# Attention and expert layer on one core: seven products from the fourth batch on, weight sums over two plain layers, splits on ScalarE

## The chip, the cores and the metric

One Trainium2 chip, one core of it. The time is device microseconds of one execution, the median of several runs. A trace of one profiled execution of the kernel before is at hand; its own time stands beside its span in the table below.

## What is computed

Eight batches of attention with a sigmoid in place of the softmax, then one expert: a product into 2048 columns, an ELU, and a product back to 768.

```python
B, H, S, D = 8, 12, 448, 64            # q, k, v
scores = q @ k.T / sqrt(D) - log(S)    # per batch and head
attn_out = sigmoid(scores) @ v         # x: 3584 tokens x 768
h = x @ w_in                           # 768 x 2048
g = where(h > 0, h, exp(min(h, 0)) - 1)
out = g @ w_out                        # 2048 x 768
```

All inputs and outputs are f32. The kernel splits each f32 operand, scaled by a power of two, into a high and a low f16 part and adds three products (high by high, low by high, high by low).

## The kernel before

**Stages.** The work goes batch by batch. For a batch b there is an *attention stretch* (six pairs of heads, class `Pair`), then a *layer* (x by w_in and the ELU, giving g). The second product of the expert (`moe2`, g by w_out) of batch b-1 is cut into output tiles of 128 tokens by 384 columns, 16 steps of 6 matmuls each, and TensorE runs these steps between the score and value products of the attention stretch of batch b (`fill`). Of the 448 tokens of a batch 384 make three whole tiles; the last 64 of two successive batches share one tile, so the stretches of batches 2, 4, 6 hold eight output tiles (even stretches) and those of 1, 3, 5, 7 hold six (odd stretches). All instructions are issued in an order written out by hand on every engine; batch 0 and the attention of batch 1 follow the string `ORDER`, whose letters each advance one stream of work.

**Layers.** `FAST = 2`: the layers of batches 0 and 1 are plain (`Expert`, `moe1`: 16 tiles of 18 matmuls of 448 columns). From batch 2 on a layer is made of seven products of halves (`FastExpert`, `moe1_fast`: four blocks j of seven products, each of 18 matmuls of 224 columns). For these, x of a pair is evicted as 32-bit data (`evict`, L833) into the place of a part of w_in (`hold`), VectorE makes sums and differences of halves (`differences`, L840 to L859), ScalarE casts them to high parts (`rest`, L872), GpSimd or VectorE makes the low parts (`rest_low`, L878). The places of successive pairs overlap, so that an eviction waits for the low parts of the pair before. `final` scales a pair by GpSimd (L814, L818) ahead of its eviction.

**Weight sums.** The layers of seven products need sums of halves of w_in. `w_in_pieces` makes them on GpSimd in 192 steps (`make`, L342 and L345) and sends them to DRAM (`pieces`): one step every fifth letter of the hand-written order from letter 266 on, four per tile in the plain layer of batch 1, and the rest in the attention stretch of batch 2. `load_piece` brings them back, four per block.

**Preparation.** For a pair that comes some pairs later q, k and v are measured (`greatest`, L220; `greatest_qk`, L570), summed over rows by TensorE (`sums`, L198, into a bank of `pm` or `pav`), scaled (`scales`, L165 to L208 on VectorE and GpSimd, L587, L589, `value_scale` L537 to L547), split into a high part (`split_high`, L625 on GpSimd) and a low part (`split_low`, VectorE, helper line L213), transposed by a DMA (`transposed`) and, for the pair after next, loaded (`load_pair`). Four pairs are prepared in an attention stretch (pairs 1 to 4 of it), two in a layer. `split` (L623) does high and low parts on ScalarE and VectorE; the layer of batch 1 uses it already.

**Order in one pair of an attention stretch:** two score tiles and their sigmoids (L732), high parts (L762, ScalarE) and low parts (L213, VectorE) of the weights `ats`; some steps of `moe2`; the third score tile; row sums, scales and `split_high` of the prepared pair; its sigmoid; the last 64 keys of two pairs (`last_keys`); `final`; `rest` of the pair before, `split_low`, `rest_low`; loads and measurement of the next pair; the other steps of `moe2`; the value products; `evict`.

**Memory.** PSUM tiles are taken by tags: `psc` two of two banks (score tiles, and bank A of the first three blocks of a layer), `pav` one bank, `pm` three. A tile of a tag is reused when its readers have finished.

Of the kernel before, what the change touches and what calls it, by code (L numbers as in the profile page):

```python
# [47 lines left out]
def attention_ffn(  # L48
# [9 lines left out]
    nc = tc.nc  # L58
# [13 lines left out]
    FAST = 2  # L72
    MADE = 265
# [115 lines left out]
    def one_more(tag, name):  # L189
        return ps.tile([P, 512], F32, tag=tag, name=name, bufs=3 if tag == "pm" else None)  # L190
# [141 lines left out]
    unsent, made = [], [0]  # L332
    PIECE_STEPS = NJ * KC * 16

    def w_in_pieces():

        extra = xall[:, NK * 2 * S :]
        free = [extra[:, i * 4 * P : (i + 1) * 4 * P] for i in range(3)]
        ends = [extra[:, 12 * P : 14 * P], spare[:, : 2 * P]]

        def add(dst, x, y, op=ALU.add):
            nc.gpsimd.tensor_tensor(dst, x, y, op=op)  # L342

        def parts(t, hi, lo):
            nc.gpsimd.tensor_copy(hi, t)  # L345
            yield
            add(lo, t, hi, ALU.subtract)
            yield

        def two(t):  # L350
            return t[:, : 2 * P], t[:, 2 * P :]

        def send(j, c, n, hi, lo):
            def run():
                to = pieces[j * 4 + n, :, :, c]
                if lo is None:
                    nc.sync.dma_start(to, hi.rearrange("p (i x) -> p i x", i=2))
                else:
                    nc.sync.dma_start(to[:, 0], hi)
                    nc.sync.dma_start(to[:, 1], lo)  # L360
            unsent.append((made[0], run))

        for j in reversed(range(NJ)):
            for c in range(KC):
                a, b, d = free
                af, bf, df = (t.bitcast(F32) for t in free)
                (h11, l11), (h12, l12), (h21, l21), (h22, l22) = (
                    (wi[:, n, j, 0, c], wi[:, n, j, 1, c]) for n in range(4)
                )
                add(af, h21, l21)  # L370
                yield
                add(bf, af, h11, ALU.subtract)
# [3 lines left out]
                yield from parts(bf, *ends)  # L376
                send(j, c, 2, *ends)
# [6 lines left out]
                yield from parts(af, *two(d))  # L384
                send(j, c, 0, d, None)
                yield from parts(bf, *ends)
                send(j, c, 1, *ends)
                add(bf, h12, bf, ALU.subtract)
# [319 lines left out]
    class Pair:  # L708
# [166 lines left out]
        def rest_low(self):  # L875
            on = nc.vector if self.hp >= NP - 2 else nc.gpsimd
            for (hi, lo), t in self.parts_of:
                on.tensor_tensor(lo, t, hi, op=ALU.subtract)  # L878
# [873 lines left out]
```

## Time and profile before

| | us |
|---|---|
| median of three runs | 1215.45 (1214.18 to 1215.93) |
| profiled execution | 1213.94 |
| span of its trace | 1212.2 |

| engine | busy us | share | instructions |
|---|---|---|---|
| TensorE (PE) | 1130.8 | 93% | 10980 |
| VectorE (DVE) | 874.4 | 72% | 1378 |
| ScalarE (ACT) | 729.0 | 60% | 955 |
| GpSimd (POOL) | 566.8 | 47% | 885 |

The mean granted TensorE clock is 0.979 of full. Busy shares are means over stages with different limits, so the rows below are read stage by stage; "idle before" is the idle time of an engine just ahead of an instruction, with what released it.

### The profile page before, as it was taken

Reading aid. Unit: us, or ns where it says so; the run is one execution under the profiler, and the core shown is the slowest. Engines: PE = TensorE matmul, PEld = TensorE weight load, DVE = VectorE, ACT = ScalarE, POOL = GpSimd, SP = SyncE. Lnnn points to the kernel's source line nnn. Section 1 sums busy time; section 2 is a strip of 40 time slices with the busy share of each in tenths; the row PEclk is TensorE's granted clock in tenths of the full one; section 3 lists DMA queues with packets and bytes.
Section 4 is the critical chain, followed back from the end, with each engine's and each line's share of the span. In section 5 each row is a group of like instructions: output and inputs, shape, how many; then the busy total and the mean of one; then the engine's idle time right before and its main releaser. Section 6 shows DMA issues by size and latency. Waiting matters only on the chain.

```text
span 1212.2 us, 26930 instructions
## 1 busy us (share of the span) xinstructions
PE 1130.8 (93%) x10980; PEld 772.1 (64%) x10980; DVE 874.4 (72%) x1378; ACT 729.0 (60%) x955; POOL 566.8 (47%) x885
## 2 busy tenths in 40 slices
PE   7889888899969999889999999889999999899998
PEld 4334454455636995559766796549866697458965
DVE  4999958967567776787767786787777876766610
ACT  6879758767555466555755557555665467565600
POOL 2357668958967234642356342562236433640000
PEclk9989999999989999999999999999999999999999
DMA  9967554343144551346224552446424462214200
GB/s 275 277 195 217 135 129 106 79 99 87 34 109 95 167 135 38 89 126 178 65 60 93 164 144 47 92 93 174 121 48 93 125 195 47 62 36 151 66 27 27
DMA packets 240044, 136.37 MB, mean 113 GB/s; under 512 B 185008, under 2 KB 217392, under 8 KB 239920
## 3 DMA queue, kind: packets, MB, share of 16 engines
q1 hardware_dynamic: 238848, 134.33, 42.0%
q8 instruction: 86, 1.41, 0.5%
q10 hardware_dynamic: 1072, 0.33, 0.1%
q14 instruction: 38, 0.31, 0.1%
HBM read 98.04 MB, written 17.30 MB: 95 GB/s over the span
## 4 chain that ended last, share of the span: by engine, by line
PE 45%; POOL 18%; DVE 15%; ACT 11%; issue 6%; DMA 4%; SPq 2%; POOLq 0%; DVEq 0%; ACTq 0%
PE po L1238 10%; PE C L1080 6%; PE a L1080 5%; POOL nat L625 5%; PE E L1080 5%; PE ph L987 5%; ACT sg L732 4%; DVE ats L213 4%; PE po_r L1238 3%; PE B L1080 3%; POOL vn L625 3%; PE psc L725 2%; PE pav L794 2%; ACT ats L762 2%; DMA wi<-pieces 2%
## 5 line engine op out<-in xcount | busy, mean ns | idle before, releaser
L1238 PE MATMUL po<-wo,g 128*64 128x384 f16 (+1 forms) x4320 | 403.3, 333 | 0.0
L1238 PEld LDWEIGHTS <-g 128*64 128x64 f16 (+1 forms) x4992 | 302.2, 111 | 157.2 <-issue 25.8
L1080 PEld LDWEIGHTS <-wi 128*128 128x128 f16 x3024 | 287.9, 98 | 6.5 <-DMA wi<-pieces 3.3
L213 DVE SCALAR_TENSOR_TENSOR ats<-sg,ats 128x896 f16<-128x896 f32 x120 | 132.7, 1135 | 72.6 <-ACT ats L762 72.4
L732 ACT ACTIVATE sg<-psc,bias,sc 128x896 f32<-128x896 f32 x126 | 133.9, 1095 | 2.8 <-PE psc L725 2.0
L725 PE MATMUL psc<-qk 64*128 64x448 f16 x756 | 89.3, 359 | 35.8 <-ACT sg L732 35.6
L625 POOL TENSOR_SCALAR nat<-raw,sc 128x384 f16<-128x384 f32 (+1 forms) x99 | 120.2, 1229 | 0.1
L570 POOL TENSOR_TENSOR mx<-mx,half 128x2 bf16<-128x2 bf16 x42 | 24.4, 581 | 196.8 <-DVE mx L220 196.8
L987 PE MATMUL ph<-xall,wi 128*128 128x448 f16 x576 | 114.7, 360 | 0.7 <-DVE e L1013 0.7
L213 DVE SCALAR_TENSOR_TENSOR nat<-raw,sc,nat 128x384 f16<-128x384 f32 (+1 forms) x126 | 83.8, 702 | 41.0 <-POOL nat L625 37.5
L762 ACT ACTIVATE ats<-sg 128x896 f16<-128x896 f32 x120 | 110.0, 951 | 3.5 <-PE pav L794 2.8
L213 DVE SCALAR_TENSOR_TENSOR g<-e,rr,g 128x768 f16<-128x768 f32 (+2 forms) x112 | 91.3, 851 | 16.5 <-ACT g L1144 15.6
L833 ACT ACTIVATE wi<-pav,sc 128x448 f32<-128x448 f32 x30 | 19.0, 634 | 137.6 <-POOL xall L878 87.8
L987 PEld LDWEIGHTS <-wi 128*128 128x128 f16 x576 | 56.3, 100 | 56.8 <-issue 8.3
L725 PEld LDWEIGHTS <-qk 64*128 64x128 f16 x756 | 32.3, 95 | 82.6 <-issue 64.1
L794 PEld LDWEIGHTS <-vn 128*64 128x64 f16 x880 | 52.2, 111 | 49.1 <-issue 18.8
L794 PE MATMUL pav<-ats,vn 128*64 128x448 f16 x720 | 78.8, 358 | 4.9 <-DVE ats L213 2.8
L169 POOL TENSOR_SCALAR sc<-sc 128x3 f32<-128x3 f32 (+1 forms) x48 | 13.9, 290 | 145.6 <-DVE pw L205 145.3
L1080 PE MATMUL C<-xall,wi 128*128 128x224 f16 x720 | 76.9, 259 | 2.3 <-DMA wi<-pieces 2.1
L1080 PE MATMUL a<-xall,wi 128*128 128x224 f16 x720 | 76.9, 259 | 0.0
L1125 ACT ACTIVATE e<-ats,msc 128x448 f32<-128x448 f32 x48 | 32.0, 666 | 62.8 <-DVE ats L1090 62.7
L1238 PE MATMUL po_r<-wo,g 128*64 128x384 f16 (+1 forms) x672 | 64.9, 326 | 0.0
(193 smaller groups left out, 1865.7 us busy)
## 6 DMA issues: line engine op xcount, KB each, us to landing
wi<-pieces SPq DMA_DIRECT2D x96, 384.0 KB, 3.6
wo<-in_moe_w_in_dram SPq DMA_DIRECT2D x8, 1536.0 KB, 7.3
raw<-in_q_dram SPq DMA_DIRECT2D x48, 192.0 KB, 3.7
rv<-in_v_dram SPq DMA_DIRECT2D x48, 192.0 KB, 3.3
raw<-in_k_dram SPq DMA_DIRECT2D x47, 192.0 KB, 3.3
out_dram<-room SPq DMA_DIRECT2D x47, 192.0 KB, 2.3
wo<-in_moe_w_out_dram SPq DMA_DIRECT2D x9, 768.0 KB, 5.4
ats<-in_moe_w_out_dram SPq DMA_DIRECT2D x6, 768.0 KB, 4.7
```

The costliest lines, as they stand in the source:

```text
L213: nc.vector.scalar_tensor_tensor(lo, src, s, hi, op0=ALU.mult, op1=ALU.subtract)
L570: nc.gpsimd.tensor_tensor(mx[:, 5:14:8], mx[:, 9:10].to_broadcast([P, 2]), half, op=ALU.mult)
L625: on.tensor_scalar(to, src, s, None, op0=ALU.mult)
L725: nc.tensor.matmul(psc[:, j, :S], kk[rows[j], o], qq[rows[j], :S], start=(n == 0), stop=(n == len(parts) - 1),)
L732: nc.scalar.activation(to, psc, AF.Sigmoid, bias=bias, scale=self.s_scale)
L762: nc.scalar.mul(hi, sg, 2.0**ATOP)
L794: nc.tensor.matmul(pav[rows[j], :S], vv[i][:, 2 * NC + j if g == NC else j * NC + g], sg[k][:, j], start=(g == 0 and n == 0), stop=(g == N ...
L833: nc.scalar.mul(t[:, : 2 * HS], self.pav[:, :S], self.x_scale)
L987: nc.tensor.matmul(self.ph[f], wi[:, 2 * (f // NQ) + c // KC, f % NQ // 2, wj, c % KC, f % 2 * P :][:, :P], self.xh[c][:, xj], start=(n == ...
L1080: nc.tensor.matmul(bank[:, u * HS : (u + 1) * HS], wi[:, w, at, wj, c, u * P : (u + 1) * P], self.x.piece(x, c, xj), start=begins and u == ...
L1125: nc.scalar.activation(e, h, AF.Exp, scale=self.scale_of(0, j, n))
L1238: nc.tensor.matmul(po[r, :HM], tokens[:, r], wo[:, i, f, wj], start=(n == 0), stop=(n == 3 * NF - 1),)
```

## The change

- `FAST = 3`: the layer of batch 2 and its attention stretch become plain.
- The 192 weight steps leave the hand-written order. A class `Pieces` makes them for given units of 16 steps on a given engine: two units on GpSimd and two on VectorE in the layer of batch 1, four on GpSimd in the attention stretch of batch 2 (one step to every second step of `moe2`), two on GpSimd and two on VectorE in the layer of batch 2. GpSimd's units have one pair of buffers for parts to be sent, VectorE's five (in `ats`).
- The splits of q, k and v go from GpSimd (`split_high`, `split_low`) to `split`, with the high parts on ScalarE; in the attention stretch they come behind the casts of x (`rest`).
- `differences` follows `evict` at once, where it stood ahead of the casts a pair later; the last two pairs' `x_most` comes behind the low parts.
- In the layers of seven products `copied`, `elu`, `high`, `low`, row sums and splits are in another order; the row sums use a bank of `psc`; `load_pair` is issued at the end of a block (in an attention stretch: behind the steps of `moe2`).
- The first pair of a stretch takes 24 steps of `moe2`, and none are kept for behind the last pair.
- In even batches k is loaded ahead of q, so that the last 64 tokens stand at the front of g, and g of every batch is written in one run; the shared output tile reads its two halves from two places.

```diff
-    FAST = 2
-    MADE = 265
+    FAST = 3
     def one_more(tag, name):
+        if tag == "psc":
+            return ps.tile([P, 2, 512], F32, tag=tag, name=name, bufs=2)[:, 0]
...
+    class Pieces:
+        def step(self, n=1):
+            for _ in range(min(n, self.left)):
+                next(self.run, None)
+                self.left -= 1
+                self.flush(self.left + 1 if self.left else -1)
...
+    few = places(xall[:, NK * 2 * S :], 3) + [(xall[:, -2 * P :], spare)]
+    many = places(at, 8)
+    on_pool = [
+        Pieces(nc.gpsimd, [(j, c, few) for j, c in units])
+        for units in (((3, 2), (2, 2)), ((2, 0), (2, 1), (1, 0), (1, 1)), ((0, 1), (0, 2)))
+    ]
+    on_dve = [
+        Pieces(nc.vector, [(j, c, many) for j, c in units])
+        for units in (((3, 0), (3, 1)), ((1, 2), (0, 0)))
+    ]
...
-        for i, src in enumerate((q, k)):
+        for i, src in enumerate((q, k) if b % 2 else (k, q)):
...
         def rest(self):
-            self.differences()
             for (hi, _), t in self.parts_of:
                 nc.scalar.copy(hi, t)
-            self.x_most()
+            if self.hp < NP - 2:
+                self.x_most()
...
-            self.runs = [(0, 0, S)] if b % 2 == 0 else [(0, 0, SM), (SM, SM + R, R)]
+            self.runs = [(0, R if b % 2 else 0, S)]
...
@@ moe1_fast
             if was:
                 x.second_first(j - 1)
                 x.exponential(j - 1, 1, 0)
+                if now:
+                    x.copied(j)
                 x.missing(j - 1, 1)
                 x.elu(j - 1, 0, 0)
                 x.elu(j - 1, 0, 1)
...
+            x.product(j, 5)
+            load(j, 0)
+            if j == 1:
+                beside("scales")
             x.product(j, 6)
             load(j, 1)
-            if was:
-                x.low(j - 1, 1)
             x.sums(j)
+            if was:
+                x.elu(j - 1, 1, 1)
+                x.elu(j - 1, 1, 0)
+                x.high(j - 1, 1)
+            if j == 2:
+                beside("scales")
             x.product(j, 7)
...
-            if j < NJ:
-                beside(2 * j)
+            if j in (1, 2):
+                beside("split")
+            elif j == 0:
+                beside("maxima")
...
+            if j == 1:
+                beside("maxima")
             x.product(j, 4)
+            load_next()
...
+    def beside_fast(what):
...
+        if what == "scales":
+            p.sums("psc")
             p.scales()
-            p.split_high(nc.gpsimd)
...
+            p.split()
+            loads.append(prepared + 2)
...
         for n, c in enumerate(ORDER):
             next(streams[c])
-            if n > MADE and n % 5 == 0:
-                make(1)
...
+        def between(f):
+            between.turn += 1
+            if f not in (4, 5, 10, 11) and f < 14 and between.turn % 4:
+                on_dve[b - 1].step()
+            if between.turn % 2 and f < 15:
+                on_pool[2 * b - 2].step()
...
                     if left % 2 == 0:
-                        make(1)
+                        on_pool[1].step()
...
-                share = left // (NP - hp) + (2 if hp == 0 else 0)
-                tail = 4 if hp == NP - 1 else 0
+                share = 24 if hp == 0 else left // (NP - hp)
+                fast = b >= FAST
+                tail = 0 if hp == NP - 1 else 0
...
                     preparation[prepared].scales()
-                    preparation[prepared].split_high(nc.gpsimd)
...
                 if works:
-                    preparation[prepared].split_low()
+                    preparation[prepared].split()
...
-                    load_pair(prepared + 2)
+                    loads.append(prepared + 2)
...
-                if hp == 2 and b == FAST:
-                    make(max(PIECE_STEPS - made[0], 0) + 2)
...
                 fill(share - gap - tail)
+                load_next()
                 for t in range(NC + 1):
                     p.values(t)
+                if not fast:
+                    p.finish()
+                    fill(tail)
+                    continue
                 p.evict()
+                p.differences()
+                if hp == NP - 2:
+                    load_piece(0, 0)
```

## Rows read from the trace of the kernel before

**Rows 1.** Stretches: length, busy PE, PEld, DVE, ACT, POOL; TensorE's granted clock; DMA share, GB/s.
```profile
144.96:243.61 98.65, 84.84 (x858) 50.22 (x858) 80.40 (x115) 67.60 (x89) 80.30 (x123) 0.95 0.42 103
243.61:298.31 54.70, 54.70 (x294) 28.21 (x293) 37.03 (x69) 36.36 (x67) 37.57 (x70) 1.00 0.43 100
298.31:401.04 102.73, 93.06 (x1054) 56.60 (x1053) 70.28 (x101) 55.95 (x74) 75.57 (x114) 0.95 0.33 80
401.04:450.17 49.13, 48.68 (x509) 48.24 (x507) 36.19 (x65) 26.24 (x35) 17.70 (x29) 1.00 0.53 155
450.17:540.19 90.02, 80.26 (x862) 48.24 (x861) 67.53 (x101) 57.44 (x73) 44.87 (x67) 0.96 0.34 77
589.56:681.62 92.06, 90.41 (x1053) 55.42 (x1053) 69.49 (x107) 58.21 (x76) 43.93 (x67) 1.00 0.38 84
730.45:820.29 89.84, 80.08 (x862) 48.11 (x861) 67.35 (x101) 57.40 (x73) 44.88 (x67) 0.96 0.34 77
1011.14:1097.17 86.03, 78.63 (x859) 45.87 (x859) 61.38 (x90) 57.08 (x73) 36.19 (x53) 0.98 0.22 49
```

**Rows 2.** TensorE in order of time in batch 4's stretch: start, length.
```profile
610.34 7.97 PE L1238 MATMUL po<-wo,g 128*64 128x384 f16 x96
```

**Rows 3.** Groups by line and form in batch 5's stretch: busy, mean ns, idle before.
```profile
L213 DVE SCALAR_TENSOR_TENSOR ats<-sg,ats 128x896 f16<-128x896 f32 x18 | 19.0, 1088 | 11.6 <-ACT ats L762 11.6
...
L725 PE MATMUL psc<-qk 64*128 64x448 f16 x108 | 12.9, 363 | 8.0 <-ACT sg L732 8.0
...
L833 ACT ACTIVATE wi<-pav,sc 128x448 f32<-128x448 f32 x5 | 3.2, 634 | 21.4 <-POOL xall L878 13.6 <-POOL sc L818 5.8 <-PE pav L794 2.0
```

**Rows 4.** Batch 5's stretch in order of time, GpSimd, ScalarE and TensorE.
```profile
771.01 3.55 POOL L625 TENSOR_SCALAR nat<-raw,sc 128x384 f16<-128x384 f32 x3
774.53 1.56 POOL L625 TENSOR_SCALAR vn<-rv,sc 128x512 f16<-128x512 f32 x1
776.07 1.03 POOL L878 TENSOR_TENSOR xall<-wi,xall 128x448 f16<-128x448 f32 x1
...
777.13 0.63 ACT L833 ACTIVATE wi<-pav,sc 128x448 f32<-128x448 f32 x1 [4.28 <-POOL xall L878]
...
778.80 0.74 PE L725 MATMUL psc<-qk 64*128 64x448 f16 x6 [2.86 <-ACT sg L732]
```

**Rows 5.** Groups by line and form, whole span: splits and measurement.
```profile
L625 POOL TENSOR_SCALAR nat<-raw,sc 128x384 f16<-128x384 f32 x66 | 96.6, 1463 | 0.1
...
L625 POOL TENSOR_SCALAR vn<-rv,sc 128x512 f16<-128x512 f32 x33 | 53.5, 1620 | 0.0
...
L220 DVE TENSOR_REDUCE mx<-raw 128x7 bf16<-128x896 f32 x42 | 45.2, 1075 | 0.0
...
L220 DVE TENSOR_REDUCE mx<-rv 128x4 bf16<-128x512 f32 x48 | 32.4, 676 | 14.9 <-DMA rv<-in_v_dram 14.9
...
L625 POOL TENSOR_SCALAR nat<-raw,sc 128x128 f16<-128x128 f32 x33 | 25.1, 760 | 0.0
...
L623 ACT ACTIVATE nat<-raw,sc 128x384 f16<-128x384 f32 x18 | 10.9, 604 | 11.2 <-POOL sc L169 11.2
...
L623 ACT ACTIVATE vn<-rv,sc 128x512 f16<-128x512 f32 x7 | 5.0, 710 | 0.2 <-PE pr L198 0.2
...
L623 ACT ACTIVATE nat<-raw,sc 128x128 f16<-128x128 f32 x9 | 3.6, 395 | 2.4 <-POOL sc L587 2.4
```

**Rows 6.** Source lines of a weight step and the nearest VectorE form: ns min/median/max.
```profile
L342 POOL TENSOR_TENSOR xall<-xall x48: 669/730/1581, 107.5 to 359.6; 128x256 f32<-128x256 f32 x24, 128x256 f16<-128x256 f32 x24
...
L840 DVE TENSOR_TENSOR wi<-wi x18: 391/393/806, 324.2 to 1066.5; 128x224 f32<-128x224 f32 x18
```

**Rows 7.** Batch 1's stretch in order of time, VectorE, TensorE and ScalarE.
```profile
161.66 0.62 DVE L1252 TENSOR_SCALAR room<-po,osc 128x384 f32<-128x384 f32 x1 [5.09 <-POOL osc L1290]
...
164.25 0.20 PE L198 MATMUL pr<-mx,x_ones 128*64 128x12 bf16 x2 [4.43 <-POOL mx L570]
...
168.14 0.97 ACT L623 ACTIVATE nat<-raw,sc 128x384 f16<-128x384 f32 x2 [7.19 <-POOL sc L169]
```

More of the change, by code (lines that the diff above doesn't have):

```diff
@@ L330, in w_in_low, with __init__, flush, send @@
             yield
[L332 to L353, printed above, removed]
+    class Pieces:
+        def __init__(self, on, units):
+            self.on, self.units = on, units
+            self.made, self.unsent, self.turn = 0, [], 0
+            self.left = 16 * len(units)
+            self.run = self.steps()
+        def step(self, n=1):
[3 more added lines that the diff above has]
+                self.flush(self.left + 1 if self.left else -1)
+        def flush(self, older=-1):
+            while self.unsent and self.unsent[0][0] > older:
+                self.unsent.pop(0)[1]()
+        def send(self, j, c, n, hi, lo):
             def run():
                 to = pieces[j * 4 + n, :, :, c]
[L356 to L366, printed above, removed]
+                nc.sync.dma_start(to[:, 0], hi)
+                nc.sync.dma_start(to[:, 1], lo)
+            self.unsent.append((self.left, run))
+        def steps(self):
+            before = None
+            for j, c, where in self.units:
+                af, bf, df = (t.bitcast(F32) for t in where[:3])
+                outs = where[3:]
                 (h11, l11), (h12, l12), (h21, l21), (h22, l22) = (
@@ L375, in w_in_pieces @@
                 yield
-                yield from parts(bf, *ends)
-                send(j, c, 2, *ends)
+                yield from parts(2, bf)
                 add(df, h22, l22)
@@ L383, in w_in_pieces, with places @@
                 yield
[L384 to L388, printed above, removed]
+                yield from parts(0, af)
+                add(df, h12, bf, ALU.subtract)
                 yield
-                add(bf, bf, l12)
+                add(df, df, l12)
                 yield
-                yield from parts(bf, *two(a))
-                send(j, c, 3, a, None)
-                free = [b, d, a]
+                yield from parts(1, bf)
+                before = parts(3, df)
+            self.flush()
+            yield from before
+    at = ats.rearrange("p a i j s -> p (a i j s)")
+    def places(t, n):
+        t = [t[:, i * 4 * P : (i + 1) * 4 * P] for i in range(n)]
+        return t[:3] + [(x[:, : 2 * P], x[:, 2 * P :]) for x in t[3:]]
+    few = places(xall[:, NK * 2 * S :], 3) + [(xall[:, -2 * P :], spare)]
[8 more added lines that the diff above has]
+    ]
     def load_piece(j, n):
@@ L895, in last_keys @@
                     nc.tensor.matmul(
-                        psc[rows[j ^ i], i, :S], kk[rows[j], o], qq[rows[j], :S],
+                        psc[rows[j ^ i], i, :S], kk[rows[j], p.last], qq[rows[j], p.tokens],
                         start=(n == 0), stop=(n == terms - 1),
@@ L1195, in moe1_fast @@
             x.exponential(j, 1, 1)
+            if was:
+                x.low(j - 1, 0)
+                x.low(j - 1, 1)
             x.product(j, 2)
@@ L1572, in attention_ffn, with measure, load_next @@
     prepared = AHEAD
+    loads, measured = [], set()
+    def measure():
+        p = preparation.get(prepared)
+        if p is not None and prepared not in measured and prepared > AHEAD:
+            measured.add(prepared)
+            p.greatest()
+            p.greatest_qk()
+    def load_next():
+        while loads:
+            load_pair(loads.pop())
     def beside(f):
         nonlocal prepared
+        if f in (6, 12):
+            load_next()
         p = preparation.get(prepared)
```

124 lines of the change are left out of this document (63 added, 61 removed).

## Prediction

> **What bounds the kernel now.** I read the granted clock and the page's busy shares first: one core, TensorE busy 93% of the span, so the question is where it stands idle or runs cold. The table of stretches answers it [rows 1]. A layer (the first product of the experts) is set by TensorE: layer 1, plain, 54.70 us with TensorE busy for all of it; layer 2, in seven products, 49.13 with 48.68 busy. The attention stretches are not alike. An even one (batch 4, with eight output tiles) takes 92.06 with TensorE busy 90.41 at full clock. An odd one (batch 5, six output tiles) has 191 matmuls fewer and still takes 89.84. An output tile of 96 matmuls costs 7.97 [rows 2], so the odd stretch should need 90.41 - 2 x 7.97 = 74.5; some 15 us are lost there. Busy 80.08 against 74.5 says how: 9.8 us of idle, and 5.6 us of matmuls at a lower clock (0.96).
>
> The groups by line of that odd stretch name the wait [rows 3]: TensorE waits 8.0 us for a sigmoid before a score product; ScalarE is idle 21.4 us before its eviction of x (L833), 13.6 of them until GpSimd's low parts of the pair before (L878) and 5.8 until its scale (L818). ScalarE works only 57.40 of 89.84 us. One place in order of time [rows 4]: GpSimd splits q and k from 771.01 to 774.56 and v to 776.09, only then comes L878, to 777.10; ScalarE's eviction waits for it 4.28 us, the sigmoids queue behind the eviction, and TensorE stands 2.86 us. So the bound is GpSimd's queue, passed on through ScalarE's order, not any engine's total.
>
> **The change part by part**, against the profiled run's own 1213.94 us (span 1212.2; the median of the runs shown is 1.5 above it).
>
> *Splits back on ScalarE.* A pair's high parts cost GpSimd 2 x 1.463 + 0.760 + 1.620 = 5.31 us and ScalarE 2 x 0.604 + 0.395 + 0.710 = 2.31 [rows 5]. In an odd stretch four pairs are prepared: GpSimd loses 21 of 44.88 us, and L878 and L818 no longer stand behind it; ScalarE goes from 57.40 to 66.6. With the differences issued right behind the eviction, the casts no longer wait for VectorE's low parts of another pair. What is late next: TensorE at 74.5; VectorE, busy 67.35, keeps the 11.6 us in which it waits for ScalarE's high part of the weights, since sigmoid, high, low stay in their order [rows 3]: together 79.0. I take 79 for batches 3 and 5 (now 90.02 and 89.84) and 77 for batch 7 (86.03; its VectorE is busy 61.38, and only three pairs are prepared). That gives -11.0 - 10.8 - 9.0 = -30.8. Ends: 74.5 each (-42.3); and the case in which ScalarE is rid of the wait for L878 alone: 66.6 + (89.84 - 57.40 - 13.6) = 85.4, some 84 for batch 7 (-11). In the even stretches TensorE's 90.41 leaves little: -1.0 each for batches 4 and 6, between 0 and -1.7: -2.0.
>
> *Seven products one batch later.* Layer 2 becomes plain: 54.70 for 49.13, +5.6. Nothing hides it, since TensorE is the bound in both. Stretch 2 gains from it: no 32-bit x, no differences, no L878, but an eviction by two plain steps, so ScalarE has nothing left to wait for at L833. Its matmuls are those of the even stretch (1054 against 1053), so the floor is 90.4, now 102.73. Against it stand 64 of the 192 weight steps, all on GpSimd here, at 0.73 [rows 6] to 1.00 us, the first what one step takes and the second the pace at which they are issued, every twelfth matmul of the output (7.97 / 96 x 12). That is 47 to 64 us, and each part must be sent out before the single pair of buffers for them is written again. The scales of a pair queue behind some ten steps; ScalarE's splits wait for these scales, but a pair here has 90.4 / 6 = 15.1 us of TensorE work and (55.95 + 9.2) / 6 = 10.9 of ScalarE, which leaves 4. I take 92.5: -10.2, between -12.3 and 0.
>
> *Weight steps out of the hand-written order.* In stretch 1 GpSimd is busy 80.30 of 98.65 us. VectorE waits 5.09 us there for the output scale that stands behind weight steps, and TensorE 4.43 us right after it for a maximum [rows 7]. These steps are gone, so 4.4 come back, and I add 1 for the scales that queue in the same way: -5.5, between 0 (VectorE, busy 80.40, sets the stretch anyway) and -9 of the 13.8 in which TensorE is idle. In layers 1 and 2 VectorE gets 32 steps each. None of its rows has this form; the nearest, 128x224, takes 0.393 [rows 6], so 256 columns some 0.45: 14 us on 37.03, 51 of 54.70, without what g in one run takes off. Cover holds, thinly: 0, between 0 and +3 a layer.
>
> *Order within the layers of seven products.* SP's loads of q, k, v move behind the load of the fourth piece; what TensorE idles in such a layer, 49.13 - 48.68 = 0.45 us in layer 2 [rows 1], can be no more than this. Against it: the row sums now take the bank of `psc` whose last readers are the ELU steps of the second-last block, and in block 2 these stand behind a split and a measurement on VectorE (0.676 + 1.075 = 1.75 us [rows 5], moved into block 1). TensorE's wait there has no row; I bound it by 0 and the 1.75 us that are put in front of it, and take 1.5, since VectorE is the later of the two in that block. The four steps of output kept until now for the end of a stretch (4 of 16 in a tile, 2.0 us) also go; two products of the layer that need nothing of the last pair stand there instead, so 0, or part of the upper end. Four such waits (the last layer prepares nothing), less 0.45 for each of the five layers where SP's order may end a wait, 6.0 - 2.3, some +3.5 for the five layers, between -2.3 and +9. In the stretches the loads of the next pair move on SP behind the sends of the output tiles; the pair is measured one pair later, so 0.
>
> *g in one run, keys and tokens changing places, the last rest tiles in halves:* fewer instructions on ScalarE and VectorE, the same columns on TensorE: 0, hidden by TensorE in the layers.
>
> **Sum:** -30.8 - 2.0 + 5.6 - 10.2 - 5.5 + 3.5 = -39.4. 1213.94 - 39.4 = 1174.5, and 1.5 more for the median: **1176 us**.
>
> **The rivals.**
> (a) ScalarE becomes the wall of the odd stretches: it loses the wait for L878 and keeps the others, 85.4, 85.4 and 84 as above: 20 us worse, 1196. For it: in the pairs with the last keys ScalarE has as much to do as TensorE. Against: 19.4 of its 32.4 idle us are the waits for L878 and L818 [rows 3], and both come from one queue that gets shorter by 5.31 us a pair.
> (b) GpSimd's single pair of buffers and 64 steps keep stretch 2 at 102.7: 1186. For it: GpSimd is busy 75.57 there now with fewer steps. Against: only the scales of four pairs depend on it.
> (c) Slower: ScalarE, in order, now stands at the splits until GpSimd's scale has come. The place: between the casts of x and the next eviction. The price: 7.2 us each, as ScalarE waits once in stretch 1 for a scale [rows 7]. An odd stretch then needs 66.6 + 4 x 7.2 = 95, an even one 58.21 + 9.2 + 28.8 = 96, and stretch 2 gains nothing. Against now: +5.6 + 5.4 + 5.6 + 8.3 - 5.5 + 3.5 = +23, 1238. It decides from some 6 us a pair, where the odd stretches are back at 90. Against it: before the scale GpSimd has no split any more in the odd and even stretches, and the third score tile's sigmoid, high parts and casts lie ahead of the split on ScalarE.
> (d) VectorE and GpSimd shut each other out in the plain layers, now that both carry weight steps: 51 + (37.57 - 32 x 0.73) = 65 for 54.7, +10 a layer, 1196. Against: layer 1 now has 37.03 + 37.57 = 74.6 of both in 54.70 without an idle TensorE, so they overlap [rows 1]. The Trainium skill (SBUF — State Buffer, Who interferes with whom) states this as a rule: a VectorE instruction with two SBUF inputs and a GpSimd one that reads SBUF hold the shared ports exclusively, and the later one blocks. By that rule the sum would be (d); layer 1's row bears it out at most in part, as steps of 0.67 us that at times take 1.5 [rows 6].
>
> **How the numbers follow.** Forecast 0.60, (a) 0.15, (b) 0.11, (d) 0.03: all faster, 0.89. (c) 0.08, slower. That gains and losses cancel to within 0.2% (2.4 us, about what a measurement can tell from no change): 0.03. The ends of all terms together reach from 1152 to 1225, but they don't fall together; to hold 8 in 10 the range takes in (a), (b) and (d) and about half the way to the floors: 1158 to 1200.
>
> **What would show it.** Right: L833 in an odd stretch waits for TensorE's values, not for L878; TensorE's clock there is near 1.00; stretches 3 and 5 take 76 to 82; stretch 2 under 95; layer 2 at 54.7; osc no longer waited for in stretch 1. Wrong: ScalarE waiting at L623 for GpSimd's scales (c), TensorE waiting for sigmoids with ScalarE over 90% busy (a), row sums waiting over 2 us in block 2 of a layer of seven products.

## The result, and the profile after

| | before | after |
|---|---|---|
| median, us | 1214.82 (1213.33 to 1215.93) | 1139.88 (1138.76 to 1141.65) |
| profiled execution, us | 1213.94 | 1140.35 |
| span of its trace, us | 1212.2 | 1138.5 |
| TensorE busy, us | 1130.8 | 1111.7 |

The ratio is 0.9385 (0.9368 to 0.9402): 75 us less. I had forecast 39 less. The direction and several terms were right; the size was not, and 1139.88 lies below the forecast's range and below its sum of all good ends (1152).

The stretches and layers of the trace after (columns as in [rows 1]; these lines answer it): batch 0's layer, stretches 1 and 2, layer 2, stretch 3, layer 3, stretches 4, 5 and 7.

```profile
78.26:139.25 60.99, 60.43 (x316) 29.23 (x316) 58.40 (x86) 55.33 (x70) 20.52 (x32) 0.97 0.64 185
139.25:218.76 79.51, 78.15 (x859) 47.76 (x858) 68.55 (x115) 66.21 (x89) 22.59 (x52) 1.00 0.41 98
273.45:363.67 90.22, 90.22 (x1053) 55.35 (x1052) 67.28 (x95) 60.15 (x80) 62.61 (x97) 1.00 0.38 91
363.67:418.37 54.70, 54.70 (x294) 28.21 (x293) 44.59 (x86) 34.04 (x54) 30.96 (x59) 1.00 0.36 87
418.37:494.32 75.95, 75.33 (x861) 44.52 (x861) 57.55 (x96) 62.76 (x87) 27.26 (x56) 1.00 0.38 84
494.32:544.55 50.23, 48.86 (x509) 48.17 (x508) 38.13 (x70) 30.21 (x44) 8.04 (x22) 1.00 0.69 178
544.55:634.77 90.22, 90.22 (x1053) 55.33 (x1053) 64.04 (x102) 64.99 (x88) 22.08 (x50) 1.00 0.35 83
683.29:758.52 75.23, 74.96 (x861) 44.42 (x861) 60.91 (x98) 64.46 (x88) 23.13 (x50) 1.00 0.35 77
948.15:1023.64 75.49, 75.18 (x859) 44.32 (x858) 58.61 (x91) 62.79 (x84) 19.74 (x41) 1.00 0.20 48
```

Compare the first number (length) with the second (TensorE busy). Before, an odd stretch was 7 to 10 us longer than the time in which TensorE was busy; now every stretch shown is within 1.4 us of it, at a clock of 1.00. Batch 0's layer, which I had not shown, was this in the kernel before, and VectorE's low parts of the weights in its stretch 1 were these (groups by line and form: busy, mean ns, idle before):

```profile
78.54:144.96 66.42, 62.64 (x317) 29.75 (x316) 64.30 (x86) 55.60 (x70) 49.64 (x61) 0.94 0.63 179
```
```profile
L213 DVE SCALAR_TENSOR_TENSOR ats<-sg,ats 128x896 f16<-128x896 f32 x12 | 16.0, 1362 | 0.0
```

Groups of the trace after: stretch 1 (three lines, answering [rows 7] and the row above), then batch 3's stretch, an odd one (three lines, answering [rows 3]; L214 is the old L213, L647 the old L623, L789 the old L762, L860 the old L833, L905 the old L878).

```profile
L214 DVE SCALAR_TENSOR_TENSOR ats<-sg,ats 128x896 f16<-128x896 f32 x12 | 12.7, 1084 | 0.0
...
L1291 DVE TENSOR_SCALAR room<-po,osc 128x384 f32<-128x384 f32 x5 | 3.1, 610 | 0.4 <-POOL osc L1329 0.4
...
L647 ACT ACTIVATE nat<-raw,sc 128x384 f16<-128x384 f32 x10 | 6.0, 603 | 3.4 <-DMA out_dram<-room 2.3 <-POOL sc L168 1.1
...
L214 DVE SCALAR_TENSOR_TENSOR ats<-sg,ats 128x896 f16<-128x896 f32 x18 | 19.2, 1099 | 12.5 <-ACT ats L789 12.4
...
L860 ACT ACTIVATE wi<-pav,sc 128x448 f32<-128x448 f32 x5 | 3.1, 630 | 7.8 <-PE pav L821 5.0 <-POOL sc L845 1.6 <-POOL xall L905 1.2
...
L752 PE MATMUL psc<-qk 64*128 64x448 f16 x108 | 12.3, 351 | 0.0
```

In stretch 1 the waits for GpSimd's scales are all but gone, and the same 12 instructions of VectorE take 1084 ns for 1362. In the odd stretch ScalarE's eviction waits 7.8 us for 21.4, mostly for TensorE's values, and TensorE no longer waits for a sigmoid. One wait has grown: in layers 3 and 5 TensorE waits for the weight pieces (its waits in layer 5, first in the kernel before, then after: in total, times, longest). TensorE's idle time went from 0.5 to 1.4 us in layer 3 and from 1.4 to 2.0 in layer 5.

```profile
PE C L1080 <- DMA wi<-pieces: 1.2, 1, 1.2
PE B L1080 <- DMA wi<-pieces: 0.3, 1, 0.3
```
```profile
PE B L1108 <- DMA wi<-pieces: 1.6, 1, 1.6
PE C L1108 <- DMA wi<-pieces: 0.5, 1, 0.5
```

The spans' difference by stages, beside the terms of the forecast:

| stages | before | after | measured | forecast |
|---|---|---|---|---|
| batch 0's layer and stretch 1 | 165.07 | 140.50 | -24.6 | -5.5 |
| stretches 3, 5, 7 | 265.9 | 226.7 | -39.2 | -30.8 |
| stretch 2 | 102.73 | 90.22 | -12.5 | -10.2 |
| layer 2, now plain | 49.13 | 54.70 | +5.6 | +5.6 |
| stretches 4, 6 | 184.1 | 180.5 | -3.7 | -2.0 |
| layers 3 to 7 and the end | 312.0 | 313.0 | +1.0 | +3.5 |
| start | 78.5 | 78.3 | -0.3 | 0 |
| sum | | | -73.7 | -39.4 |

More than half of the miss of 34.3 us is the first line, a quarter the second.

### The profile page after: what moved, and what is told of

Read it like the earlier page. It is cut to its first block, busy times and chain, and to the rows that moved or that the text cites. A ratio compares the mean times of both kernels' runs of the same rounds, so it can differ in the third digit from the quotient of the medians.

```text
span 1138.5 us, 26741 instructions
## 1 busy us (share of the span) xinstructions
PE 1111.7 (98%) x10860; PEld 741.4 (65%) x10860; DVE 833.5 (73%) x1382; ACT 781.8 (69%) x1050; POOL 334.2 (29%) x678
## 4 chain that ended last, share of the span: by engine, by line
PE 78%; DVE 8%; ACT 5%; DMA 4%; issue 2%; SPq 1%; POOL 1%; ACTq 0%; DVEq 0%
PE po L1277 26%; PE ph L1015 12%; PE psc L752 6%; PE E L1108 6%; PE pav L821 6%; PE a L1108 6%; PE C L1108 6%; PE po_r L1277 6%; PE B L1108 3%; ACT sg L759 1%; DVE ats L214 1%; DMA wo<-in_moe_w_in_dram 1%; DVE ar L778 1%; DMA rv<-in_v_dram 1%; PE pscr L923 1%
## 5 line engine op out<-in xcount | busy, mean ns | idle before, releaser
L1108 PEld LDWEIGHTS <-wi 128*128 128x128 f16 x2520 | 240.1, 98 | 6.2 <-DMA wi<-pieces 4.4
L214 DVE SCALAR_TENSOR_TENSOR ats<-sg,ats 128x896 f16<-128x896 f32 x120 | 131.4, 1123 | 76.1 <-ACT ats L789 75.9
L1015 PE MATMUL ph<-xall,wi 128*128 128x448 f16 x864 | 167.4, 355 | 0.1
L1015 PEld LDWEIGHTS <-wi 128*128 128x128 f16 x864 | 83.7, 98 | 80.6 <-issue 5.1
L789 ACT ACTIVATE ats<-sg 128x896 f16<-128x896 f32 x120 | 109.7, 947 | 0.7
L214 DVE SCALAR_TENSOR_TENSOR g<-e,rr,g 128x896 f16<-128x896 f32 (+1 forms) x80 | 77.7, 991 | 13.0 <-ACT g L1172 12.7
L214 DVE SCALAR_TENSOR_TENSOR nat<-raw,sc,nat 128x384 f16<-128x384 f32 (+1 forms) x126 | 70.5, 607 | 7.4 <-ACT nat L647 7.0
L821 PEld LDWEIGHTS <-vn 128*64 128x64 f16 x880 | 50.3, 110 | 34.3 <-issue 4.1
L647 ACT ACTIVATE nat<-raw,sc 128x384 f16<-128x384 f32 (+1 forms) x126 | 60.5, 532 | 17.2 <-POOL sc L168 9.1
L1172 ACT ACTIVATE g<-e,rr 128x896 f16<-128x896 f32 x40 | 41.0, 1036 | 38.4 <-DVE e L1163 31.3
L1108 PE MATMUL C<-xall,wi 128*128 128x224 f16 x600 | 64.1, 259 | 0.6 <-DMA wi<-pieces 0.6
L1277 PE MATMUL po_r<-wo,g 128*64 128x384 f16 x768 | 64.4, 327 | 0.0
L1108 PE MATMUL a<-xall,wi 128*128 128x224 f16 x600 | 64.1, 259 | 0.0
L778 DVE SCALAR_TENSOR_TENSOR ar<-sgr,ar 64x448 f16<-64x448 f32 x80 | 58.8, 735 | 2.5
```

The source lines that it names most:

```text
L214: nc.vector.scalar_tensor_tensor(lo, src, s, hi, op0=ALU.mult, op1=ALU.subtract)
L647: nc.scalar.mul(to, src, s)
L778: nc.vector.scalar_tensor_tensor(ar[of[1 - j], j], sg[r, i], 2.0**ATOP, ar[r, j], op0=ALU.mult, op1=ALU.subtract,)
L789: nc.scalar.mul(hi, sg, 2.0**ATOP)
L821: nc.tensor.matmul(pav[rows[j], :S], vv[i][:, 2 * NC + j if g == NC else j * NC + g], sg[k][:, j], start=(g == 0 and n == 0), stop=(g == N ...
L1015: nc.tensor.matmul(self.ph[f], wi[:, 2 * (f // NQ) + c // KC, f % NQ // 2, wj, c % KC, f % 2 * P :][:, :P], self.xh[c][:, xj], start=(n == ...
```

## Experiments

Stage times are those of each kernel's profiled execution, times of whole kernels are medians. "After" is 1139.88 us; the kernel before, timed beside the other kernels, took 1210.85 to 1215.19, so a few us between two whole kernels say little. Nor does a single us in a layer of seven products: six of the kernels (the one after, four with extra instructions in the hand-written order, one with all weight steps on GpSimd) have the same code from batch 3 on, and there layer 3 took 49.2 to 52.8 us and layer 5 49.5 to 50.9. The odd stretches of these six agree within 0.5 us.

**The hand-written part: GpSimd's queue, or two engines that read SBUF at once?** Four kernels put instructions back on GpSimd, in the kernel after, at the 100 places where weight steps had stood (one at each place, two with the long fills); nobody reads what they write.

```
 for n, c in enumerate(ORDER):
     next(streams[c])
+    if n > 265 and n % 5 == 0:
+        nc.gpsimd.tensor_tensor(da, da, db, op=ALU.add)      # additions
+        # fills:       nc.gpsimd.memset(<128x768 f32>, 0.0)
+        # long fills:  that, and nc.gpsimd.memset(<128x192 f32>, 0.0)
+        # casts:       nc.gpsimd.tensor_copy(<128x256 f16>, da)
```

> The changed kernel, with 100 additions put on GpSimd (128x256 f32, two SBUF operands, a scratch that nobody reads) at the places in the hand-written order where the kernel before made 100 of its weight steps. It tests whether the 24.6 us that batch 0's layer and batch 1's stretch lost (66.46 + 98.65 before, 60.99 + 79.51 after) come from the weight steps on GpSimd alone. If they do, by either theory below: these two stages go back up by 15 to 25 us, to 156 to 165 us, the time to 1155 to 1165, and VectorE's busy time in batch 1's stretch rises from 68.6 towards 80. Rival: the new order of the loads (k before q) and of g did it: under 1143.

> The same 100 places, each with a fill of 128x768 f32 on GpSimd (about 0.74 us by the fill of 128x128, 0.204 us, less 0.1 us of start), which only writes SBUF and reads nothing. The queue on GpSimd is as long as with the additions. Theory 1, stretching: GpSimd's and VectorE's instructions that both read SBUF hold each other up, VectorE's total grows and the stretch with it; fills don't: the time stays under 1146, and VectorE's busy time in batch 1's stretch at 68 to 70. Theory 2, the queue: scales stand behind the weight steps on GpSimd and VectorE, ScalarE and TensorE stand behind the scales; then fills cost as much as additions, 1155 to 1165, with VectorE idle before the output scale as before (5.09 us).

> The changed kernel with a fill of 128x768 and one of 128x192 f32 on GpSimd at each of the 100 places of the hand-written order, some 0.743 + 0.26 = 1.0 us a place, so that GpSimd is busy as long as with the additions (88.6 us in batch 1's stretch), and still reads nothing. The shorter fills cost 9.5 us in batch 0's layer and batch 1's stretch, the additions 32.4. If the additions cost more only because they keep GpSimd's queue longer (0.957 us each for 0.743): both stages together at 165 to 175 us here. If what costs is that both engines read SBUF at once: 150 to 158, VectorE's busy time in the stretch still 68 to 70 us and its low parts of the weights at 1.08 us.

> At the same 100 places one cast of 128x256 f32 to f16 on GpSimd, which reads one SBUF operand and writes SBUF (a quarter of the weight steps were such casts, 0.713 us each in batch 1's stretch of before). If one operand read is enough to stretch VectorE's two-operand instructions: its busy time in batch 1's stretch 74 to 84 us and both stages together 160 to 173 us. If it takes GpSimd's second operand: as with the short fills, 148 to 153 us and VectorE at 68 to 70.

| on GpSimd, mean us each in stretch 1 | whole kernel | batch 0's layer | stretch 1 | both, over after |
|---|---|---|---|---|
| nothing (after) | 1139.88 | 60.99 | 79.51 | |
| fills, 0.743 | 1148.95 | 61.34 | 88.62 | +9.5 |
| casts, 0.608 | 1150.31 | 63.38 | 87.88 | +10.8 |
| long fills, 0.741 + 0.264 | 1161.34 | 62.35 | 97.90 | +19.8 |
| additions, 0.957 | 1172.22 | 68.94 | 103.97 | +32.4 |
| (weight steps of before) | | 66.42 | 98.65 | +24.6 |

Stretch 1 as a window, then VectorE's low parts and ScalarE's splits in it from the groups by line, for the additions and after them for the long fills:

```profile
149.86:253.83 103.97, 85.48 (x858) 51.03 (x858) 85.39 (x115) 67.59 (x89) 88.55 (x123) 0.93 0.33 76
```
```profile
L214 DVE SCALAR_TENSOR_TENSOR ats<-sg,ats 128x896 f16<-128x896 f32 x12 | 16.3, 1382 | 0.0
...
L647 ACT ACTIVATE nat<-raw,sc 128x384 f16<-128x384 f32 x10 | 6.1, 606 | 14.7 <-POOL sc L168 14.7
```
```profile
139.75:237.65 97.90, 82.93 (x859) 48.74 (x858) 70.75 (x115) 67.03 (x89) 82.41 (x178) 0.95 0.34 80
```
```profile
L214 DVE SCALAR_TENSOR_TENSOR ats<-sg,ats 128x896 f16<-128x896 f32 x12 | 12.8, 1084 | 0.2 <-ACT ats L789 0.2
...
L647 ACT ACTIVATE nat<-raw,sc 128x384 f16<-128x384 f32 x10 | 6.1, 607 | 16.9 <-POOL sc L168 16.9
```

The same row of VectorE's with the short fills and with the casts:

```profile
L214 DVE SCALAR_TENSOR_TENSOR ats<-sg,ats 128x896 f16<-128x896 f32 x12 | 12.7, 1084 | 0.0
```
```profile
L214 DVE SCALAR_TENSOR_TENSOR ats<-sg,ats 128x896 f16<-128x896 f32 x12 | 14.2, 1208 | 0.0
```

Instructions on GpSimd at these places bring the loss back and more, so nothing else in the change is needed to explain the 24.6 us. Both theories hold a part. The short fills cost more than theory 1 allowed and less than theory 2 asked; the long ones, at 160.3 us for the two stages, lie between my two bands; the casts have the time of the one outcome and, with VectorE busy 72.8 us, a part of the other.

Fills leave VectorE's low parts at 1084 ns however long they are. What they cost is the queue: scales and maxima stand behind them on GpSimd (ScalarE waits 16.9 us for scales with the long ones). Fills about as long as an undisturbed weight step (L342 took 0.73 us in the median [rows 6]) cost 9.5; about as long as one of these additions, 10.3 more; the additions, which read two operands, another 12.6, and there VectorE is busy 85.4 us for 70.8. The casts read one operand and already stretch VectorE's low parts to 1208 ns. So, as an estimate, some 60% of the additions' loss is queue (19.8 of 32.4), half of that because reading makes the steps themselves longer, and 40% is VectorE slowed. The split is rough, since GpSimd is busy 82.4 us with the long fills and 88.6 with the additions. In stretch 1 it is 18.4 and 6.1; in batch 0's layer 1.4 and 6.6, the 1.4 within what that layer varies by among kernels that leave it alone (60.7 to 62.3).

For the weight steps of before these shares were not measured by an edit, but TensorE's waits in stretch 1 of that trace show both parts:

```profile
PE pr L198 <- POOL mx L570: 5.3, 2, 4.4
PE psc L725 <- ACT sg L732: 2.3, 2, 1.9
PE pav L794 <- DVE xall L213: 2.1, 1, 2.1
PE pav L794 <- DVE ats L213: 1.5, 2, 0.8
PE pav L794 <- DVE ar L751: 1.0, 2, 0.7
```

It waited 5.3 us for maxima and 4.6 for VectorE's low parts. With the long fills the two are 10.2 and 1.1 us, with the additions 7.7 and 6.5, in the kernel after 0 and 0.6.

**The odd stretches: where GpSimd's splits stood in the queue, or that they were GpSimd's at all?** Three kernels give the high parts of q, k, v back to GpSimd in stretches 3 to 7 of the kernel after, at three places; a fourth takes the kernel before and moves only the splits.

```
 split_on_gpsimd        behind scales():      split_high(nc.gpsimd); split() -> split_low()
 split_behind_low       behind rest_low():    split_high(nc.gpsimd); split_low()
 split_nobody_waits     behind rest_low():    split_high(nc.gpsimd)
                        behind differences(): split_low(); load_next()
 before_split_on_scalar (kernel before) no split_high(nc.gpsimd); split_low() -> split()
```

> The changed kernel with the high parts of q, k and v back on GpSimd in the attention stretches of batches 3 to 7, right behind their scales, and the low parts where the splits now stand; all else as changed. If GpSimd's queue was the bound of the odd stretches (my prediction's step): they go from 75.5 back to 85 to 90 us, L905's low parts are waited for again before the eviction, the clock drops below 1.00, and the time is 1170 to 1185. If the new place of the differences carried the gain: odd stretches under 79, the time under 1150.

> The changed kernel with the high parts of q, k and v on GpSimd in the stretches of batches 3 to 7, but issued behind the low parts of x (L905) instead of ahead of them. GpSimd has the same work as in the run with the splits right behind the scales (odd stretches 88.3, 90.0, 85.6), only the order of its queue differs. Theory 1, the queue ahead of L905: the eviction no longer waits for a split, the odd stretches come back to under 79 us, the time to 1140 to 1152. Theory 2, stretching (VectorE busy 62.6 us there for 57.6 with the splits on ScalarE): the odd stretches stay over 84, the time over 1165. In between, each has the share that the odd stretches show.

> The changed kernel with the high parts of q, k and v on GpSimd in the stretches of batches 3 to 7, behind the low parts of x (L905) as in the run before, and now with their low parts on VectorE moved to the end of the pair, behind the differences, so that VectorE needn't stand for them (there it stood 16.1 us in batch 3's stretch, the maxima came late and TensorE waited 8.3 us for them). GpSimd does the same work in all three runs. If waiting in the order of an engine is the bound of the odd stretches, whichever engine it is: 75 to 79 us each, the time 1140 to 1152. If GpSimd's reading itself holds VectorE up (stretching): still over 83 each, the time over 1162, with VectorE's busy time over 62.

> The kernel before with one part of the change alone: in the attention stretches the high and low parts of q, k and v are made where the low parts stood, the high ones on ScalarE. Differences, loads and all else as before. If the splits alone carry the odd stretches: these go from 90.0, 89.8 and 86.0 to 77 to 81, stretch 2 from 102.7 to under 98, and the time to 1170 to 1180. If they need the new place of the differences and loads too: odd stretches over 83, the time over 1185. The hand-written part (165.1 us for batch 0's layer and batch 1's stretch) must not move by over 1 us.

| us | whole kernel | stretch 3 | 5 | 7 | 4 | 6 |
|---|---|---|---|---|---|---|
| before | 1214.82 | 90.02 | 89.84 | 86.03 | 92.06 | 92.06 |
| after | 1139.88 | 75.95 | 75.23 | 75.49 | 90.22 | 90.23 |
| split_on_gpsimd | 1181.69 | 88.26 | 89.95 | 85.63 | 92.01 | 91.85 |
| split_behind_low | 1187.13 | 89.13 | 89.92 | 87.83 | 91.18 | 91.18 |
| split_nobody_waits | 1181.90 | 85.21 | 86.49 | 85.45 | 95.57 | 98.52 |
| before_split_on_scalar | 1175.21 | 79.94 | 79.98 | 77.19 | 90.33 | 90.33 |

The wait that carries it, in batch 3's stretch: first with the splits behind the scales, then behind the low parts of x, then with their own low parts put off as well.

```profile
L860 ACT ACTIVATE wi<-pav,sc 128x448 f32<-128x448 f32 x5 | 3.2, 634 | 32.0 <-POOL xall L905 19.8 <-POOL sc L845 7.5 <-PE pav L821 4.7
...
L752 PE MATMUL psc<-qk 64*128 64x448 f16 x108 | 12.4, 352 | 10.0 <-ACT sg L759 10.0
```
```profile
L214 DVE SCALAR_TENSOR_TENSOR nat<-raw,sc,nat 128x384 f16<-128x384 f32 x8 | 7.0, 880 | 14.1 <-POOL nat L649 14.1
...
L860 ACT ACTIVATE wi<-pav,sc 128x448 f32<-128x448 f32 x5 | 3.2, 635 | 19.6 <-PE pav L821 11.3 <-POOL sc L845 6.4 <-POOL xall L905 1.9
...
L199 PE MATMUL pr<-mx,x_ones 128*64 128x12 bf16 x8 | 0.8, 188 | 8.3 <-POOL mx L594 8.3
```
```profile
L923 PE MATMUL pscr<-qk 64*64 64x448 f16 x36 | 3.6, 420 | 5.6 <-DMA qk<-nat 5.6
...
L214 DVE SCALAR_TENSOR_TENSOR ats<-sg,ats 128x896 f16<-128x896 f32 x18 | 19.2, 1096 | 15.0 <-ACT ats L789 15.0
```

The splits alone, in the kernel before, carry most of the gain. The odd stretches come out as expected, and so does stretch 2 (under 98), which loses 8.4 of its 12.5 us although its layer is still one of seven products (stretches 2 and 3):

```profile
302.03:396.33 94.30, 91.92 (x1054) 56.15 (x1053) 65.42 (x102) 64.16 (x90) 55.09 (x97) 0.98 0.36 87
445.31:525.25 79.94, 76.89 (x861) 46.24 (x860) 62.99 (x101) 64.73 (x89) 23.66 (x51) 1.00 0.38 85
```

One condition failed: the hand-written part, which that edit leaves alone, took 167.4 us for 165.1. So batch 0's layer and stretch 1 together vary by some 2 us from run to run.

Put back right behind the scales, the splits on GpSimd take nearly the whole gain of the odd stretches away, in the way that the forecast's step has it (L905 waited for 19.8 us, the clock 0.98 in batch 3's stretch). But the place in GpSimd's queue, which I had named as the cause, is not enough. Behind the low parts the eviction waits 1.9 us for L905, and the stretch is as long as ever, because VectorE now stands 14.1 us for the high parts, measures late, and TensorE waits 8.3 us for maxima. With the low parts put off too, the odd stretches are still 85 to 86 us: in batch 3's TensorE waits 5.6 us for q and k themselves, and its clock there is 0.96 (busy 77.80 us, 75.33 after), the other part of the loss.

By times alone the second and third kernel fit the outcome that I had written down for GpSimd's reading, but the traces speak against it. In batch 3's stretch VectorE is busy 58.4 us in the second and 60.7 in the third, for 57.6 after, and its low parts of the weights take 1099 and 1096 ns for 1099.

What remains is that the cost follows the length of the split on the way from a pair's scales to its scores, by whichever wait comes last. That is argued, not shown. The third kernel also moved the low parts to the end of the pair, its even stretches grew as well (95.57 and 98.52, TensorE waiting for q and k there too), and no kernel had ScalarE's short splits at that late place.

**The place of the differences.** Two kernels put `differences` back ahead of the casts; the second also puts the first piece's load back behind `rest_low`. In the first, that load overwrites values that the late differences still read, so it computes a wrong x in the last pairs and only its times are used.

```
     def rest(self):
+        self.differences()
...
             p.evict()
-            p.differences()
```

> The changed kernel with the differences of x back ahead of the casts, a pair later than the eviction; splits stay on ScalarE. If the splits carried the gain of the odd stretches: these stay within 1.5 us of 75.5 each, the time 1140 to 1145. If the place of the differences carried it: ScalarE waits at the casts for VectorE again (10.5 us a stretch before), odd stretches of 80 us and more, the time over 1153.

> As the run with the differences ahead of the casts, with the first piece's load put back behind the low parts of the last pair, so that it can't overwrite what the late differences still read (there the odd stretches took 78.5, 78.4 and 76.7, layers 3 and 5 some 6 us more than with the differences early). If the place of the differences costs by itself: odd stretches 77 to 79 (ScalarE waits some 5 us a stretch for L867 at the casts), and layers 3 and 5 at 55 to 57, since the pieces are sent for late in both; the time 1158 to 1168. If the 6 us a layer came from that one load's place: layers 3 and 5 under 52, the time under 1152.

The first took 1168.56 us, the second 1155.79; stretches 3, 5 and 7 took 78.54, 78.39, 76.65 and 78.58, 78.76, 76.64, layers 3 and 5 56.50, 57.11 and 52.91, 50.71. ScalarE's casts in batch 3's stretch of the second, and TensorE's wait in its layer 3:

```profile
L899 ACT CAST xall<-wi 128x448 f16<-128x448 f32 x5 | 2.8, 562 | 5.2 <-DVE wi L867 5.2
```
```profile
PE C L1109 <- DMA wi<-pieces: 2.6, 1, 2.6
```

The differences' place is worth 2.6, 3.5 and 1.2 us in the three odd stretches (7.3 in all), with ScalarE waiting 5.2 us at the casts. For the first kernel that lies between my two outcomes: more than 1.5 us in two of the three stretches, but under 80 us in all. In the second, layer 3 fell between my two bands, and close to what it took in the kernel with the additions, whose differences are early (52.84); layer 5 fell into the lower, and the time between the two. So most of the 6 us of the first kernel belonged to the piece's load.

**Weight steps without VectorE.** `on_dve` is left without units; its four go to GpSimd's in layers 1 and 2, a step at every place of the interleaving.

> The changed kernel with all weight steps on GpSimd: 64 in each of the plain layers 1 and 2 (one at every place of the interleaving) and the 64 of stretch 2 as they are; VectorE makes none. It tests whether spreading them over VectorE matters, and rival (d), that the two engines hold each other up in the plain layers. In layers 1 and 2 GpSimd would need 64 times 0.73 to 1.0, 47 to 64 us, of 54.7. If TensorE hides it: both layers 54.7 and the time 1139 to 1142. If scales and row sums queue behind the steps: layers of 57 to 65, the time 1145 to 1160.

1146.68 us. Layer 1, stretch 2 and layer 2, then ScalarE's splits and TensorE's row sums in stretch 2:

```profile
219.86:274.55 54.69, 54.69 (x293) 28.20 (x293) 30.81 (x55) 33.70 (x53) 38.47 (x71) 1.00 0.35 82
274.55:370.74 96.19, 91.09 (x1053) 57.12 (x1052) 65.06 (x91) 58.85 (x80) 70.67 (x111) 1.00 0.39 93
370.74:426.20 55.46, 55.04 (x293) 28.04 (x292) 33.38 (x59) 34.27 (x54) 44.75 (x80) 1.00 0.30 74
```
```profile
L650 ACT ACTIVATE nat<-raw,sc 128x384 f16<-128x384 f32 x8 | 4.9, 607 | 23.2 <-POOL sc L168 23.2
...
L199 PE MATMUL pr<-mx,x_ones 128*64 128x12 bf16 x8 | 0.8, 189 | 3.9 <-POOL mx L597 3.9
```

The layers are those of my first outcome, 54.7 and 55.5, the time that of the second, and it is stretch 2 that pays, 96.2 for 90.2. GpSimd finished 49 of its 64 steps in layer 1; the others run on into the stretch, and ScalarE stands 23.2 us there for scales (8.0 in the kernel after). VectorE's share of the weight steps is worth that, 6 to 7 us, which no term of the forecast held.

**Two versions against the wait for the pieces.** `pieces_first` issues no loads of q, k, v in the last two pairs of a stretch from batch 3 on (`load_next` only for `hp < NP - 2`); `low_parts_early` moves `rest`, `rest_low` and the loads of pieces 1 and 2 behind the last pair's first two sigmoids.

> A version that may beat the changed kernel: in the last two pairs of a stretch of batch 3 or later the loads of q, k and v for a later pair are not issued; they go out at the end of the layer's first block instead. SP then issues the loads of the weight pieces about 5 us earlier; TensorE waited 1.4 and 2.0 us for these at the start of layers 3 and 5. If SP's order is what keeps them: layers 3 and 5 go from 50.2 and 50.9 to 48.6, the time to 1135 to 1138. If the pieces wait for the casts and low parts of x in whose place they land: no change, 1139 to 1141. If the later loads hold up the measurement in block 1: slower, over 1142.

> A second version that may beat the changed kernel: in the last pair of a stretch of batch 3 or later the casts and low parts of the pair before come right behind the first two sigmoids, and the loads of pieces 1 and 2 behind them, some 5 us earlier. The run with the loads of q, k and v out of the way showed that these loads then wait 5.8 us for L905. If that is all that keeps them: layers 3 and 5 at 48.6 to 49.2 and odd stretches unchanged, the time 1135 to 1138. If ScalarE and VectorE, now later with the weights of the last pair, hold up its values: the odd stretches grow by 1 us or more and the time stays at 1139 or more.

1140.12 us (1137.74 to 1144.64) and 1141.17 us (1140.55 to 1143.92): neither beats the kernel after. In the traces layers 3 and 5 took 52.55 and 49.34 us with the first version, 48.52 and 48.51 with the second. SP's waits in the first, around layer 3, and in the second TensorE's waits in batch 3's stretch:

```profile
SPq L421 <- DVE xall L905: 5.8, 1, 5.8
```
```profile
PE pav L821 <- DVE ar L778: 0.6, 2, 0.3
PE pav L821 <- DVE ats L214: 0.6, 1, 0.6
```

Out of the way of other loads, the pieces wait for the low parts of x in whose place they land (5.8 us for 1.3 in the kernel after). With those made early, layers 3 and 5 wait no longer, and stretches 3 and 5 take 78.3 and 77.6 for 76.0 and 75.2: the last pair's weights are late instead. The wait has only moved.

## Why the prediction was right or wrong

- **Weight steps out of the hand-written order** (forecast -5.5, ends 0 and -9; measured -24.6): the step that failed. I counted one direct wait of TensorE for a maximum, 4.4 us, and 1 us for others like it. The trace of before held 4.6 us more of waits for VectorE's low parts and 2.3 for sigmoids. TensorE's idle time in stretch 1 fell from 13.8 to 1.4 us, not by 4.4 to 9; its matmuls, 858 and 859 in the rows, took 78.15 us for 84.84 as the granted clock rose from 0.95 to 1.00, and I had counted that loss in the odd stretches but not here; and batch 0's layer, with GpSimd busy 49.6 of 66.4 us, stood in no term at all, though it gained 5.4. My reason for the lower end, VectorE busy 80.40 us, took VectorE's time as its own: some 12 us of it, 80.40 less 68.55 for 115 instructions in both, came with GpSimd's work beside it; the additions alone bring VectorE from 68.55 to 85.39.
- **Odd stretches** (79, 79, 77; measured 75.95, 75.23, 75.49). The splits alone give 79.94, 79.98 and 77.19. That this meets the term within 1 us is luck, for the working that led to 79 is refuted: it added VectorE's 67.35 us of work and its wait of 11.6 for high parts. With the splits alone VectorE is busy 62.99 us in batch 3's stretch and waits 9.4, together 72.4 and not the stretch; in the kernel after it is busy 57.55 and waits 12.5, with TensorE idle for 0.6 us. The early differences add 2.6, 3.5 and 1.2 us, and I gave them nothing of their own. The cause was too narrow as well: GpSimd's queue ahead of L878 is one way by which the split on GpSimd costs time, not the only one.
- **Layer 2** (+5.6; measured +5.6): right. **Stretch 2** (-10.2 and its end of -12.3; measured -12.5): the size was near, the reason only in part. I put the gain down to the plain layer, but the splits alone give 8.4 us of it. GpSimd's single pair of buffers (rival b) did not decide: GpSimd waits 11.5 us there for parts to be sent and ScalarE 8.0 us for scales, under TensorE's 90.22. The margin is thin: fifteen steps left over from layer 1 cost 6 us.
- **Layers of seven products** (+3.5; measured +1.0): the wait for the bank of `psc`, four times 1.5 us in my sum, is absent; TensorE's idle time for late pieces, which I had not named, grew by 0.8 us in layer 3 and 0.6 in layer 5. Both are less than these layers vary by.
- **Even stretches** (-2.0; measured -3.7): both now last as long as their matmuls.
- **Rivals.** (a) ScalarE as the wall: refuted, it is busy 62.8 of 76.0 us. (c) ScalarE waiting for scales: 0.7 us at L647 in batch 3's stretch; its price appears only where GpSimd is full (stretch 2 with all weight steps on it, stretch 1 with fills or additions). (d) VectorE and GpSimd slowing each other: real, but not in the plain layers, where I put it; these last 54.70 with both at work. The Trainium skill (SBUF — State Buffer, Who interferes with whom) says that a VectorE instruction with two SBUF inputs contends with a GpSimd one that reads SBUF and not with one that only writes it. By the rows of stretch 1 the trace agrees: 1084 ns beside fills, 1208 beside casts, 1382 beside additions. I had weighed the rule only where TensorE covers it, and not where it set the time.
- **The range.** Its lower end, 1158, was said to go half the way to the floors; from 1176 to 1152 it goes three quarters of it.

Still open: from the splits alone to the kernel after the odd stretches lose another 4.0, 4.8 and 1.7 us, of which the early differences explain 2.6, 3.5 and 1.2; the rest, 0.5 to 1.4 us, lies in the later loads, the moved measurements or g in one run, and was not told apart. For the weight steps themselves the shares of queue and slowing are known only from the waits above, and that the length of the split carries the odd stretches is not shown.

## What to carry to other kernels

Here work taken off an engine that shares its queue and its memory access with others was worth several times the one wait that I had read from the path. So list all waits of the bound engine in a stage, compare the mean time of the same instruction with and without its neighbour, and count the clock in every stretch that has idle time. When a slow step sits on the way from one stage to the next, moving it in the queue may only rename the wait, as it did here; try to shorten the step. A wait of an engine that is not the bound is no term of the sum.

## What the runs showed of the hardware

- VectorE's 128x896 low part takes 1.08 us beside GpSimd's fills of either length, 1.21 beside casts and 1.38 beside additions.
- A GpSimd instruction of one column is not constant either: the scale L845 took 0.44 us on average in batch 3's stretch of the kernel after and 1.43 with the splits on GpSimd and nobody waiting.

```profile
L845 POOL TENSOR_SCALAR sc<-sc,ratio 128x1 f32<-128x1 f32 x3 | 4.3, 1429 | 0.3
```

- TensorE's granted clock fell where it was idle: in stretch 1 it was 1.00 with 1.4 us idle (after), 0.95 with 13.8 (before) and 0.93 with 18.5 (additions). The sum of idle time does not settle it: with the splits back on GpSimd it was 0.98 in batch 3's stretch with 10.7 us idle (right behind the scales), and 0.94 in batch 5's with 6.8 (low parts put off too).
